# Mixture of experts behind attention: 624 slots per expert instead of 640

## Chip, cores and metric

One core of a Trainium2 chip runs the whole program. The metric is the device time of one execution in microseconds, as the median of several runs. Engines are named as the profile names them: PE (TensorE, with its weight loads PEld), DVE (VectorE), ACT (ScalarE), POOL (GpSimd) and SP (SyncE, which issues most DMAs).

## The reference

Three layers on 2304 tokens of 512 features: an attention that goes through 32 memory slots a head, a dense layer pair with an ELU between (512 to 2048 to 512), and a mixture of 8 experts with a noisy choice of two for each token.

```python
logits = x @ w_gate
noise_scale = np.log1p(np.exp(x @ w_noise))
noisy_logits = logits + noise_scale * noise
top2 = np.argpartition(-noisy_logits, 2, axis=1)[:, :2]
...
for e in range(E):
    for k in range(2):
        mask = top2[:, k] == e
        h = np.maximum(x[mask] @ w1[e], 0.0)          # 512 -> 1024
        out[mask] += top2_w[mask, k, None] * (h @ w2[e])  # 1024 -> 512
```

2304 tokens with two experts each make 4608 rows for 8 experts, 576 for one on average.

## The kernel before

The work is a flat list of units, each cut into slices of the hidden layer 128 wide (an iteration of the main loop). Units 0 to 3 are the dense layer pair on 576 tokens each, with 16 slices; the attention of the next block and the gating of the last one are woven between their matmuls. The rest are expert units with 8 slices. Experts 0 to 3 have two units each: a first one of 256 slots (E0A), filled from the first two blocks of tokens alone so that it can start early, and later one of the other CAP - 256 = 384 slots. Experts 4 to 7 have one unit of CAP = 640 slots each. The order is: four units of 256, four of 384, four of 640.

A slot is a row of a list in DRAM (`lst`, 2304 rows per expert, each a token number and a weight). The gating computes for every token its expert and its position there, and GpSimd scatters the pair into the list (line 643). The lists are first filled with numbers of junk rows (lines 842 to 846, 869), so that an unused slot reads and writes rows that nobody needs. `fetch` (L689) reads a unit's list and gathers its rows of x2d tile by tile, 128 slots each; `spread` (L710) turns each tile with four transposes on TensorE and splits it into a high and a low part for float32r (`halve`).

In each iteration `layer1` (L733) computes 128 hidden features for all slots of the unit: three terms (low x high, high x low, high x high) times four pieces of the 512 features, 12 matmuls for each stretch of at most 512 slots. A unit of 640 is cut in two halves of 320 (`splits`), so it has 24. `relu_` (L766) then splits the result again. Two iterations later (LAG) `layer2` (L775) takes each tile of 128 slots as the stationary operand and streams 512 output columns, three matmuls a tile, summed in one PSUM bank a tile over the 8 slices. `put_rows` (L790) scales a finished tile by the slots' weights and scatter-adds it to the output.

The order is written by hand; each engine runs its own queue in program order. SP loads the experts' weights as 1024 KB for two slices into three buffers, ACT and DVE split them into high and low parts. An expert that draws more tokens than CAP gets tiles of 128 slots behind everything, in a loop whose count is computed on the chip (`overflow_table`, and the loop at L987).

Of the kernel before, what the change touches and what calls it, by code (L numbers as in the profile page):

```python
# [9 lines left out]
F32 = mybir.dt.float32  # L10
F32R = mybir.dt.float32r
BF16 = mybir.dt.bfloat16
I32 = mybir.dt.int32
# [12 lines left out]
NT = N // P  # L26

BLOCKS = [(0, 4), (4, 5), (9, 4), (13, 5)]
CAP = 640
CT = CAP // P  # L30

NA, E0A = 4, 256
TPE = N // P
JUNK = 1024
NOV = 32
LAG = 2
# [4 lines left out]
def moe_stack_kernel(ctx, tc, phi, kv, q, wmlp, wgn, noise, wmoe, out):  # L41
# [16 lines left out]
    wxa = dr.tile([16, P, 512], F32, name="wxa")  # L58
    wxb = dr.tile([16, P, 512], F32, name="wxb")
    x2d = dr.tile([N + JUNK, DM], F32, name="x2d")  # L60
    lst = dr.tile([NE * N + P, 2], I32, name="lst")
    tabd = dr.tile([NOV, 2], I32, name="tabd")

    def bank(tag="px", bufs=1):
# [459 lines left out]
    def gating(blk, rows):  # L524
# [115 lines left out]
        for tt in range(nt):  # L640
            for k in range(2):
                pool.memset(tiny, 0.0)
                d = pool.indirect_dma_start(
                    out=lst[:NE * N], out_offset=bass.IndirectOffsetOnAxis(ap=slot[:, tt, k:k + 1], axis=0),
                    in_=rec[:, tt, k], in_offset=None)
# [6 lines left out]
    def overflow_table():  # L652
        tot = att["tot"]
        nti = sm.tile([1, NE], I32, tag="o_nti", name="o_nti")
        ntf = sm.tile([1, NE], F32, tag="o_ntf", name="o_ntf")
        end = sm.tile([1, NE], F32, tag="o_end", name="o_end")
        ge = sm.tile([1, NOV, NE], F32, tag="o_ge", name="o_ge")
        res = sm.tile([1, NOV, 2], F32, tag="o_res", name="o_res")
        tab = sm.tile([1, NOV, 2], I32, tag="o_tab", name="o_tab")
        cnt = sm.tile([1, 1], I32, tag="o_cnt", name="o_cnt")  # L660
        dve.tensor_scalar(ntf, tot[0:1], -float(CAP), 0.0, op0=OP.add, op1=OP.max)
        dve.tensor_scalar(ntf, ntf, 127.0, None, op0=OP.add)
        dve.tensor_copy(nti, ntf)
# [12 lines left out]
        dve.tensor_tensor(ge, ge, ntf[:, None, :].to_broadcast([1, NOV, NE]), op=OP.mult)  # L676
        dve.tensor_reduce(out=res[:, :, 1], in_=ge, axis=AX, op=OP.add)
        yield "light"

        dve.tensor_tensor(res[:, :, 1], ii, res[:, :, 1], op=OP.subtract)  # L680
        dve.tensor_scalar(res[:, :, 1], res[:, :, 1], float(CT), None, op0=OP.add)
        dve.scalar_tensor_tensor(res[:, :, 1], res[:, :, 0], float(TPE), res[:, :, 1], op0=OP.mult, op1=OP.add)
        dve.tensor_scalar(res[:, :, 0], res[:, :, 0], float(NE - 1), None, op0=OP.min)
        dve.tensor_scalar(res[:, :, 1], res[:, :, 1], float(NE * TPE - 1), None, op0=OP.min)
        dve.tensor_copy(tab, res)
        sp.dma_start(tabd[None], tab)
        att["cnt"] = cnt
        yield


    def fetch(n, wait=0, after=4):

        for _ in range(wait):
            yield "next"
        mp = moe["pool"]
        rows = JUNK + (BLOCKS[2][0] * P if n["early"] else N)
        ids = mp.tile([P, 5, 2], I32, tag="ids", name="ids", bufs=6)
        a, nt = n["e"] * N + n["s0"], n["nt"]
        sp.dma_start(ids[:, :nt], lst[a:a + nt * P].rearrange("(t p) c -> p t c", p=P))
        n["ids"] = ids  # L700
        n["xg"] = []
        for tt in range(nt):
            xg = mp.tile([P, DM], F32, tag="xg", name="xg", bufs=12)
            pool.indirect_dma_start(out=xg, out_offset=None, in_=x2d[:rows],  # L704
                                    in_offset=bass.IndirectOffsetOnAxis(ap=ids[:, tt, 0:1], axis=0))
            n["xg"].append(xg)
        for _ in range(after):
            yield "next"

    def spread(n):  # L710
        xt = n["x"]
        for tt in range(n["nt"]):
            bk = side_bank()
            for c in range(4):
                pe.transpose(bk[:, c * P:(c + 1) * P], n["xg"][tt][:, c * P:(c + 1) * P], ident)
            v = bk.rearrange("p (c n) -> p c n", c=4)
            hi = xt[0][:, :, tt * P:(tt + 1) * P]
            later(lambda a=(v, hi, xt[1][:, :, tt * P:(tt + 1) * P]): halve(*a))
            yield

    def new_x():
# [2 lines left out]
    def splits(u):  # L724
        if u["kind"] == "mlp":
            return [(0, S // 2), (S // 2, S // 2)]
        n = u["nt"] * P
        return [(0, n)] if n <= 512 else [(0, n // 2), (n // 2, n // 2)]

    def layer1(u, i, s0, n):  # L730
# [44 lines left out]
    def layer2(u, f, i, gh, gl, tiles=None):  # L775
        if f == 0:
            u["acc"] = [bank("acc%d" % t) for t in range(u["nt"])]
        if i >= NRAW:
            wh, wl = ready["b", i]
        for t in range(u["nt"]) if tiles is None else tiles:  # L780
            o = slice(t * P, (t + 1) * P)
            acc = u["acc"][t]
            if i < NRAW:
                pe.matmul(acc, gh.bitcast(F32)[:, o], raws["b", i], start=f == 0, stop=f == u["nf"] - 1)
                continue
            pe.matmul(acc, gl[:, o], wh, start=f == 0, stop=False)  # L786
            pe.matmul(acc, gh[:, o], wl, start=False, stop=False)  # L787
            pe.matmul(acc, gh[:, o], wh, start=False, stop=f == u["nf"] - 1)  # L788

    def put_rows(u, t, acc):  # L790
        r = rp.tile([P, DM], F32, tag="rows", name="rows")
        if u["kind"] == "mlp":
            if t % 2:
                act.activation(r, acc, AF.Copy)
            else:
                dve.tensor_copy(r, acc)
            a = JUNK + (BLOCKS[u["blk"]][0] + t) * P
            sp.dma_start(x2d[a:a + P, :], r)
            u["rows"].append(r)
        else:  # L800
            ids = u["ids"]
            wcol = ids.bitcast(F32)[:, t, 1:2]
            if t % 2:
                act.activation(r, acc, AF.Copy, scale=wcol)
            else:
                dve.tensor_scalar(r, acc, wcol, None, op0=OP.mult)  # L806
            pool.memset(tiny, 0.0)
            d = pool.indirect_dma_start(  # L808
                out=out, out_offset=bass.IndirectOffsetOnAxis(ap=ids[:, t, 0:1], axis=0), in_=r,
                in_offset=None, compute_op=OP.add)  # L810
# [14 lines left out]
    for f in at0[3:5]:  # L825
# [12 lines left out]
    dve.tensor_scalar(ecap, iota8, float(N), None, op0=OP.mult)  # L838
# [9 lines left out]
    moe_unit = lambda e, t, nt: dict(kind="moe", e=e, s0=t * P, nt=nt, nf=8, early=False)  # L848
    units += [moe_unit(e, 0, E0A // P) | dict(early=True) for e in range(NA)]
# [137 lines left out]
    with tc.For_i(0, nov, 1) as it:  # L987
        cur = mp.tile([1, 2], I32, tag="cur", name="cur")
        sp.dma_start(cur, tabd[bass.ds(it, 1), :])
        ev = sp.value_load(cur[0:1, 0:1], min_val=0, max_val=NE - 1)  # L990
        tv = sp.value_load(cur[0:1, 1:2], min_val=0, max_val=NE * TPE - 1)
        ids = mp.tile([P, 5, 2], I32, tag="ids", name="ids", bufs=6)
        sp.dma_start(ids[:, 0, :], lst.rearrange("(t p) c -> t p c", p=P)[bass.ds(tv, 1)].rearrange("a p c -> p (a c)"))
# [53 lines left out]
```

## Time and profile before

| what | value |
|---|---|
| median of 3 runs | 936.93 us (935.42 to 937.83) |
| profiled execution | 937.07 us, span 935.0 us, mean granted clock 0.979 |
| PE busy | 890.4 us (95%) |
| PE's weight loads | 736.7 us (79%) |
| DVE, ACT, POOL busy | 548.4, 455.1, 165.8 us |
| layer 2 of the experts, L786 to L788 | 3 x 544 matmuls, 218.3 + 213.2 + 213.0 us |
| layer 1 of the experts, L740 | 3 x 512 matmuls, 98.6 + 96.6 + 96.4 us |
| DMA | 153.12 MB, mean 164 GB/s |

The span is the time from the first to the last instruction; the run's own time is 2.1 us longer. Matmuls overlap: the busy time of one in the table (its mean) holds its latency, so what a matmul costs in a stream is read from the distance between two starts. The units of 256 slots begin at 443.8 us, those of 384 at 553.85, those of 640 at 691.89, and the last matmul starts at 925.00.

### The profile page before, as it was taken

What the parts mean: (1) busy time and instruction counts of PE and PEld (TensorE: products, weight loads), DVE (VectorE), ACT (ScalarE), POOL (GpSimd) and SP (SyncE); (2) the same over time, 40 slices, a digit from 0 to 9 for tenths busy, and PEclk for the clock granted to TensorE, in tenths of its full rate; (3) what the DMA queues carried; (4) which work ended last, traced back from release to release, by engine and by line L of the source; (5) the groups of instructions that cost most, each with busy time, mean ns of one, the idle gap of its engine ahead of it and who ended that gap; (6) DMA issues with size and microseconds to landing.
All of it is one profiled execution on the core that took longest, in us unless ns stands there. A gap on an engine that the chain in (4) does not pass through costs nothing. (4 is left out here: it accounts for less than half of the span.)

```text
span 935.0 us, 15299 instructions
## 1 busy us (share of the span) xinstructions
PE 890.4 (95%) x5810; PEld 736.7 (79%) x5810; DVE 548.4 (59%) x1189; ACT 455.1 (49%) x1003; POOL 165.8 (18%) x249
## 2 busy tenths in 40 slices
PE   6699999999989889999989999999999999999995
PEld 4366556787868667778878899999999999999994
DVE  4878977567577777578575654554544453442421
ACT  3676656545565556565554654444443242332310
POOL 0100100000000405033025312313304032030303
PEclk9689999999999999999999999999999999999998
DMA  8896549565652224342638966647546145162404
GB/s 318 301 360 230 181 149 357 212 237 158 210 205 90 69 72 136 118 151 53 230 96 160 309 204 191 169 138 212 145 172 180 58 113 168 46 147 74 72 3 57
DMA packets 69612, 153.12 MB, mean 164 GB/s; under 512 B 11170, under 2 KB 20130, under 8 KB 69538
## 3 DMA queue, kind: packets, MB, share of 16 engines
q1 hardware_dynamic: 59426, 131.12, 41.8%
q0 software_dynamic: 10112, 21.02, 11.6%
q8 instruction: 46, 0.75, 0.3%
q14 instruction: 28, 0.23, 0.1%
HBM read 119.42 MB, written 32.69 MB: 163 GB/s over the span
## 5 line engine op out<-in xcount | busy, mean ns | idle before, releaser
L786 PE MATMUL acc<-bh,gl 128*128 128x512 f32 x544 | 218.3, 401 | 0.6 <-DVE rows L806 0.5
L787 PE MATMUL acc<-bl,gh 128*128 128x512 f32 x544 | 213.2, 392 | 0.0
L788 PE MATMUL acc<-bh,gh 128*128 128x512 f32 x544 | 213.0, 391 | 0.0
L768 DVE SCALAR_TENSOR_TENSOR gl<-ph,gh 128x320 fp32r<-128x320 f32 (+2 forms) x128 | 62.9, 491 | 222.4 <-ACT gh L767 222.4
L470 ACT ACTIVATE bh<-raw 128x512 fp32r<-128x512 f32 x144 | 90.0, 625 | 78.1 <-PE acc L788 78.1
L788 PEld LDWEIGHTS acc<-bh,gh 128*128 128x128 f32 x544 | 102.3, 188 | 22.9
L767 ACT ACTIVATE gh<-ph 128x320 fp32r<-128x320 f32 (+2 forms) x128 | 55.8, 436 | 129.9 <-PE ph L740 129.9
L786 PEld LDWEIGHTS acc<-bh,gl 128*128 128x128 f32 x544 | 102.6, 189 | 18.7 <-DVE rows L806 1.2
L787 PEld LDWEIGHTS acc<-bl,gh 128*128 128x128 f32 x544 | 102.5, 188 | 16.6
L808 POOL DMA_INDIRECT out<-rows,ids x40 | 65.2, 1629 | 239.2 <-DVE rows L806 220.0
L476 DVE TENSOR_TENSOR bl<-raw,bh 128x512 fp32r<-128x512 f32 x144 | 98.7, 685 | 4.3 <-ACT bh L470 4.3
L740 PE MATMUL ph<-xl,ah 128*128 128x320 f32 (+2 forms) x512 | 98.6, 314 | 0.5 <-DVE gl L768 0.5
L740 PE MATMUL ph<-xh,ah 128*128 128x320 f32 (+2 forms) x512 | 96.6, 311 | 0.0
L740 PE MATMUL ph<-xh,al 128*128 128x320 f32 (+2 forms) x512 | 96.4, 310 | 0.0
L740 PEld LDWEIGHTS ph<-xl,ah 128*128 128x128 f32 x512 | 82.6, 189 | 6.7 <-DVE gl L768 0.9
L740 PEld LDWEIGHTS ph<-xh,ah 128*128 128x128 f32 x512 | 80.9, 189 | 0.0
L740 PEld LDWEIGHTS ph<-xh,al 128*128 128x128 f32 x512 | 80.7, 188 | 0.1
L740 PE MATMUL ph<-tl,fh 128*128 128x288 f32 x256 | 64.1, 332 | 11.1 <-DVE elu L754 5.5
L740 PEld LDWEIGHTS ph<-tl,fh 128*128 128x128 f32 x256 | 42.6, 195 | 37.4 <-issue 16.0
L476 DVE TENSOR_TENSOR al<-raw,ah 128x512 fp32r<-128x512 f32 x96 | 65.5, 682 | 0.0
L760 ACT ACTIVATE gh<-elu 128x576 fp32r<-128x576 f32 (+1 forms) x48 | 31.8, 662 | 66.6 <-DVE elu L754 66.6
L704 POOL DMA_INDIRECT xg<-x2d,ids x40 | 41.0, 1024 | 122.7 <-DMA ids<-lst 87.6
(219 smaller groups left out, 1290.8 us busy)
## 6 DMA issues: line engine op xcount, KB each, us to landing
raw<-in_wmoe SPq DMA_DIRECT2D x48, 1024.0 KB, 5.1
raw<-in_wmlp SPq DMA_DIRECT2D x32, 512.0 KB, 6.5
raw<-wxa SPq DMA_DIRECT2D x12, 1024.0 KB, 5.9
raw<-wxb SPq DMA_DIRECT2D x12, 1024.0 KB, 7.6
kv<-in_kv SPq DMA_DIRECT2D x8, 1024.0 KB, 11.9
out<-zrow SPq DMA_DIRECT2D x13, 512.0 KB, 8.7
q<-in_q SPq DMA_DIRECT2D x8, 576.0 KB, 8.0
x2d<-rows SPq DMA_DIRECT2D x18, 256.0 KB, 5.9
```

The source lines that it names most:

```text
L470: act.activation(ready[h, c][0], raws[h, c], AF.Copy)
L476: dve.tensor_tensor(lo, raws.pop((h, c)), hi.bitcast(F32), op=OP.subtract)
L704: pool.indirect_dma_start(out=xg, out_offset=None, in_=x2d[:rows], in_offset=bass.IndirectOffsetOnAxis(ap=ids[:, tt, 0:1], axis=0))
L740: pe.matmul(ph, w, x, start=k == 0, stop=k == len(terms) - 1)
L760: act.activation(gh[:, o], m, AF.Copy)
L767: act.activation(gh[:, o], ph, AF.Relu)
L768: dve.scalar_tensor_tensor(gl[:, o], ph, 0.0, gh[:, o].bitcast(F32), op0=OP.max, op1=OP.subtract)
L786: pe.matmul(acc, gl[:, o], wh, start=f == 0, stop=False)
L787: pe.matmul(acc, gh[:, o], wl, start=False, stop=False)
L788: pe.matmul(acc, gh[:, o], wh, start=False, stop=f == u["nf"] - 1)
L808: d = pool.indirect_dma_start(out=out, out_offset=bass.IndirectOffsetOnAxis(ap=ids[:, t, 0:1], axis=0), in_=r, in_offset=None, compute_op= ...
```

## The change

CAP becomes 624 = 4 x 128 + 112. The units of 640 slots become units of 624, in two halves of 312 and with a fifth tile of 112 slots; the units of 384 become 368, with a third tile of 112. Gathers, transposes, matmuls, scaling and scatters of these last tiles take 112 rows. The first units of 256 stay. The lists get LS = 2416 rows per expert, so that tiles of overflow, which now begin at slot 624, end inside the list of their expert; their start is kept in units of 16 rows (GR).

```diff
-CAP = 640
-CT = CAP // P
+CAP = 624
+LS = CAP + -(-(N - CAP) // P) * P
+GR = 16
...
-    lst = dr.tile([NE * N + P, 2], I32, name="lst")
+    lst = dr.tile([NE * LS, 2], I32, name="lst")
...
+    def size(u, t):
+        return min(P, u["n"] - t * P) if u["kind"] == "moe" else P
...
     def fetch(n, wait=0, after=4):
...
-        a, nt = n["e"] * N + n["s0"], n["nt"]
+        a, nt = n["e"] * LS + n["s0"], n["nt"]
...
-            pool.indirect_dma_start(out=xg, out_offset=None, in_=x2d[:rows],
-                                    in_offset=bass.IndirectOffsetOnAxis(ap=ids[:, tt, 0:1], axis=0))
+            m = size(n, tt)
+            pool.indirect_dma_start(out=xg[:m], out_offset=None, in_=x2d[:rows],
+                                    in_offset=bass.IndirectOffsetOnAxis(ap=ids[:m, tt, 0:1], axis=0))
...
     def spread(n):
...
-                pe.transpose(bk[:, c * P:(c + 1) * P], n["xg"][tt][:, c * P:(c + 1) * P], ident)
+                pe.transpose(bk[:, c * P:c * P + m], n["xg"][tt][:m, c * P:(c + 1) * P], ident[:m, :m])
...
     def splits(u):
...
-        n = u["nt"] * P
+        n = u["n"]
         return [(0, n)] if n <= 512 else [(0, n // 2), (n // 2, n // 2)]
...
     def layer2(u, f, i, gh, gl, tiles=None):
...
-            o = slice(t * P, (t + 1) * P)
-            acc = u["acc"][t]
+            m = size(u, t)
+            o = slice(t * P, t * P + m)
+            acc = u["acc"][t][:m]
...
     def put_rows(u, t, acc):
...
-            wcol = ids.bitcast(F32)[:, t, 1:2]
+            m = size(u, t)
+            r, acc, wcol = r[:m], acc[:m], ids.bitcast(F32)[:m, t, 1:2]
...
-    k = NE * TPE + 1
+    k = NE * LS // P
-    units += [moe_unit(e, E0A // P, (CAP - E0A) // P) for e in range(NA)]
-    units += [moe_unit(e, 0, CT) for e in range(NA, NE)]
+    units += [moe_unit(e, E0A, CAP - E0A) for e in range(NA)]
+    units += [moe_unit(e, 0, CAP) for e in range(NA, NE)]
...
     def overflow_table():
...
-        dve.tensor_scalar(res[:, :, 1], res[:, :, 1], float(CT), None, op0=OP.add)
+        dve.tensor_scalar(res[:, :, 1], res[:, :, 1], float(P // GR), float(CAP // GR), op0=OP.mult, op1=OP.add)
```

Every engine keeps its order; the shapes change. TensorE while expert 6 is worked on: the last two accumulators (tiles 3 and 4) of one iteration's layer 2, the transposes of expert 7's last tile of gathered rows (`xg`), and the first half of the next layer 1, before:

```order
L786 MATMUL acc_8395<-bh,gl 128x512
L787 MATMUL acc_8395<-bl,gh 128x512
L788 MATMUL acc_8395<-bh,gh 128x512
L786 MATMUL acc_8396<-bh,gl 128x512
L787 MATMUL acc_8396<-bl,gh 128x512
L788 MATMUL acc_8396<-bh,gh 128x512
L715 MATMUL px<-ident,xg 128x128 x4
L740 MATMUL ph<-xl,ah 128x320 x4
L740 MATMUL ph<-xh,al 128x320 x4
L740 MATMUL ph<-xh,ah 128x320 x4
```

The same place with the change, where the line numbers are 6 or 7 higher:

```order
L793 MATMUL acc_8395<-bh,gl 128x512
L794 MATMUL acc_8395<-bl,gh 128x512
L795 MATMUL acc_8395<-bh,gh 128x512
L793 MATMUL acc_8396<-bh,gl 112x512
L794 MATMUL acc_8396<-bl,gh 112x512
L795 MATMUL acc_8396<-bh,gh 112x512
L721 MATMUL px<-ident,xg 128x112 x4
L746 MATMUL ph<-xl,ah 128x312 x4
L746 MATMUL ph<-xh,al 128x312 x4
L746 MATMUL ph<-xh,ah 128x312 x4
```

Nothing moved: the fifth tile's three matmuls have 112 rows of output, its transposes 112 columns, and layer 1 streams 312 columns a half.

TensorE between two units of the other kind (experts 0 to 3): the transposes of a third tile, layer 1, and the first tile of layer 2, before:

```order
L715 MATMUL px<-ident,xg 128x128 x4
L740 MATMUL ph<-xl,ah 128x384 x4
L740 MATMUL ph<-xh,al 128x384 x4
L740 MATMUL ph<-xh,ah 128x384 x4
L786 MATMUL acc_6449<-bh,gl 128x512
L787 MATMUL acc_6449<-bl,gh 128x512
L788 MATMUL acc_6449<-bh,gh 128x512
```

With the change:

```order
L721 MATMUL px<-ident,xg 128x112 x4
L746 MATMUL ph<-xl,ah 128x368 x4
L746 MATMUL ph<-xh,al 128x368 x4
L746 MATMUL ph<-xh,ah 128x368 x4
L793 MATMUL acc_6449<-bh,gl 128x512
L794 MATMUL acc_6449<-bl,gh 128x512
L795 MATMUL acc_6449<-bh,gh 128x512
```

Nothing moved here either: 112 columns turned, 368 streamed in layer 1.

## Rows read from the trace of the kernel before

**Rows 1.** Busy us, share, instructions of each engine; granted clock in tenths by slice.

```profile
PE 890.4 (95%) x5810; PEld 736.7 (79%) x5810; DVE 548.4 (59%) x1189; ACT 455.1 (49%) x1003; POOL 165.8 (18%) x249
...
PEclk9689999999999999999999999999999999999998
```

**Rows 2.** Stretches: length, busy us (instructions) by engine, clock, DMA share, GB/s.

```profile
469.00:491.00 22.00, 19.41 (x114) 16.93 (x113) 17.17 (x52) 13.00 (x25) 5.68 (x15) 0.92 0.36 100
588.00:692.00 104.00, 104.00 (x546) 94.71 (x545) 53.39 (x89) 46.00 (x85) 29.08 (x32) 1.00 0.61 177
750.00:870.00 120.00, 120.00 (x684) 109.16 (x684) 46.99 (x83) 41.12 (x80) 21.68 (x25) 1.00 0.39 104
```

**Rows 3.** Waits, 553 to 915 us: total us, times, longest us.

```profile
DVE gl L768 <- ACT gh L767: 186.0, 96, 4.7
ACT gh L767 <- PE ph L740: 113.7, 95, 4.8
ACT bh L470 <- PE acc L788: 69.1, 40, 2.5
```

**Rows 4.** Waits of SyncE's queue, 553 to 915 us.

```profile
SPq L400 <- DVE bl L476: 286.9, 29, 15.6
```

**Rows 5.** TensorE in order, 640 slots: start, us, line, tiles, shape.

```profile
890.53 0.76 PE L740 MATMUL ph<-xl,ah 128*128 128x320 f32 x4
...
894.07 0.40 PE L786 MATMUL acc<-bh,gl 128*128 128x512 f32 x1
...
897.50 0.76 PE L740 MATMUL ph<-xl,ah 128*128 128x320 f32 x4
```

**Rows 6.** TensorE in order, 384 slots.

```profile
600.57 0.86 PE L740 MATMUL ph<-xl,ah 128*128 128x384 f32 x4
...
602.68 0.40 PE L786 MATMUL acc<-bh,gl 128*128 128x512 f32 x1
...
604.73 0.51 PE L740 MATMUL ph<-xl,ah 128*128 128x384 f32 x2
```

**Rows 7.** TensorE in order, 256 slots.

```profile
547.82 0.64 PE L740 MATMUL ph<-xl,ah 128*128 128x256 f32 x4
...
549.26 0.40 PE L786 MATMUL acc<-bh,gl 128*128 128x512 f32 x1
...
550.66 0.52 PE L740 MATMUL ph<-xl,ah 128*128 128x256 f32 x3
```

**Rows 8.** Weight loads by shape: count, busy us, mean ns, idle before.

```profile
L787 PEld LDWEIGHTS acc<-bl,gh 128*128 128x128 f32 x544 | 102.5, 188 | 16.6
...
L262 PEld LDWEIGHTS px<-kmT,q 128*128 128x128 f32 x80 | 9.5, 192 | 2.1 <-DMA q<-in_q 1.5 <-ACT kmT L221 0.3 <-issue 0.2
...
L262 PEld LDWEIGHTS acc<-kmT,q 128*64 128x64 f32 x24 | 1.6, 137 | 1.2 <-issue 1.1
...
L608 PEld LDWEIGHTS <-ones 128*128 128x128 bf16 x4 | 0.4, 100 | 0.0
```

**Rows 9.** TensorE in order, one tile of gathered rows turned.

```profile
746.74 0.60 PE L715 MATMUL px<-ident,xg 128*128 128x128 f32 x4
747.09 0.84 PE L740 MATMUL ph<-xl,ah 128*128 128x320 f32 x4
```

**Rows 10.** The end in order of time.

```profile
925.00 0.39 PE L788 MATMUL acc<-bh,gh 128*128 128x512 f32 x1
...
925.43 0.75 DVE L806 TENSOR_SCALAR rows<-acc,ids 128x512 f32<-128x512 f32 x1 [3.33 <-PE acc L788]
926.46 1.56 POOL L808 DMA_INDIRECT out<-rows,ids  x1 [0.49 <-DVEq L987]
```

**Rows 11.** DMA issues, 915 us to the end: count, us to landing.

```profile
out<-rows,ids POOLq DMA_INDIRECT x5, 4.9
```

**Rows 12.** The page's DMA issues: count, KB each, us to landing.

```profile
raw<-in_wmlp SPq DMA_DIRECT2D x32, 512.0 KB, 6.5
```

**Rows 13.** GpSimd in order, first 60 us.

```profile
24.95 1.05 POOL L291 TENSOR_TENSOR sb<-sb,ssu 128x512 f32<-128x512 f32 x1 [22.28 <-DVE ssu L289]
```

More of the change, by code (lines that the diff above doesn't have):

```diff
@@ L28 @@
 BLOCKS = [(0, 4), (4, 5), (9, 4), (13, 5)]
-CAP = 640
-CT = CAP // P
+CAP = 624
+LS = CAP + -(-(N - CAP) // P) * P
+GR = 16
 NA, E0A = 4, 256
-TPE = N // P
 JUNK = 1024
@@ L643, in gating @@
                 d = pool.indirect_dma_start(
-                    out=lst[:NE * N], out_offset=bass.IndirectOffsetOnAxis(ap=slot[:, tt, k:k + 1], axis=0),
+                    out=lst, out_offset=bass.IndirectOffsetOnAxis(ap=slot[:, tt, k:k + 1], axis=0),
                     in_=rec[:, tt, k], in_offset=None)
@@ L680, in overflow_table @@
         dve.tensor_tensor(res[:, :, 1], ii, res[:, :, 1], op=OP.subtract)
-        dve.tensor_scalar(res[:, :, 1], res[:, :, 1], float(CT), None, op0=OP.add)
-        dve.scalar_tensor_tensor(res[:, :, 1], res[:, :, 0], float(TPE), res[:, :, 1], op0=OP.mult, op1=OP.add)
+        dve.tensor_scalar(res[:, :, 1], res[:, :, 1], float(P // GR), float(CAP // GR), op0=OP.mult, op1=OP.add)
+        dve.scalar_tensor_tensor(res[:, :, 1], res[:, :, 0], float(LS // GR), res[:, :, 1], op0=OP.mult, op1=OP.add)
         dve.tensor_scalar(res[:, :, 0], res[:, :, 0], float(NE - 1), None, op0=OP.min)
-        dve.tensor_scalar(res[:, :, 1], res[:, :, 1], float(NE * TPE - 1), None, op0=OP.min)
+        dve.tensor_scalar(res[:, :, 1], res[:, :, 1], float((NE * LS - P) // GR), None, op0=OP.min)
         dve.tensor_copy(tab, res)
@@ L712, in spread @@
         for tt in range(n["nt"]):
-            bk = side_bank()
+            bk, m = side_bank(), size(n, tt)
             for c in range(4):
-                pe.transpose(bk[:, c * P:(c + 1) * P], n["xg"][tt][:, c * P:(c + 1) * P], ident)
-            v = bk.rearrange("p (c n) -> p c n", c=4)
-            hi = xt[0][:, :, tt * P:(tt + 1) * P]
-            later(lambda a=(v, hi, xt[1][:, :, tt * P:(tt + 1) * P]): halve(*a))
+                pe.transpose(bk[:, c * P:c * P + m], n["xg"][tt][:m, c * P:(c + 1) * P], ident[:m, :m])
+            v = bk.rearrange("p (c n) -> p c n", c=4)[:, :, :m]
+            hi, lo = (t[:, :, tt * P:tt * P + m] for t in xt)
+            later(lambda a=(v, hi, lo): halve(*a))
             yield
@@ L808, in put_rows @@
             d = pool.indirect_dma_start(
-                out=out, out_offset=bass.IndirectOffsetOnAxis(ap=ids[:, t, 0:1], axis=0), in_=r,
+                out=out, out_offset=bass.IndirectOffsetOnAxis(ap=ids[:m, t, 0:1], axis=0), in_=r,
                 in_offset=None, compute_op=OP.add)
@@ L837, in moe_stack_kernel @@
               allow_small_or_imprecise_dtypes=True)
-    dve.tensor_scalar(ecap, iota8, float(N), None, op0=OP.mult)
+    dve.tensor_scalar(ecap, iota8, float(LS), None, op0=OP.mult)
     pool.iota(ii, pattern=[[1, NOV]], base=0, channel_multiplier=0, allow_small_or_imprecise_dtypes=True)
     pool.iota(tokid, pattern=[[P, NT]], base=JUNK, channel_multiplier=1)
-    k = NE * TPE + 1
+    k = NE * LS // P
     pre = rp.tile([P, DM], F32, tag="rows", name="rows").bitcast(I32)[:, :2 * k].rearrange("p (t c) -> p t c", c=2)
@@ L847, in moe_stack_kernel @@
     units = [dict(kind="mlp", blk=k, nt=BLOCKS[k][1], nf=16) for k in range(4)]
-    moe_unit = lambda e, t, nt: dict(kind="moe", e=e, s0=t * P, nt=nt, nf=8, early=False)
-    units += [moe_unit(e, 0, E0A // P) | dict(early=True) for e in range(NA)]
-    units += [moe_unit(e, E0A // P, (CAP - E0A) // P) for e in range(NA)]
-    units += [moe_unit(e, 0, CT) for e in range(NA, NE)]
+    moe_unit = lambda e, s0, n: dict(kind="moe", e=e, s0=s0, n=n, nt=-(-n // P), nf=8, early=False)
+    units += [moe_unit(e, 0, E0A) | dict(early=True) for e in range(NA)]
+    units += [moe_unit(e, E0A, CAP - E0A) for e in range(NA)]
+    units += [moe_unit(e, 0, CAP) for e in range(NA, NE)]
     late = 4 + NA
@@ L990, in moe_stack_kernel @@
         ev = sp.value_load(cur[0:1, 0:1], min_val=0, max_val=NE - 1)
-        tv = sp.value_load(cur[0:1, 1:2], min_val=0, max_val=NE * TPE - 1)
+        tv = sp.value_load(cur[0:1, 1:2], min_val=0, max_val=(NE * LS - P) // GR)
         ids = mp.tile([P, 5, 2], I32, tag="ids", name="ids", bufs=6)
-        sp.dma_start(ids[:, 0, :], lst.rearrange("(t p) c -> t p c", p=P)[bass.ds(tv, 1)].rearrange("a p c -> p (a c)"))
+        sp.dma_start(ids[:, 0, :], lst.rearrange("(t p) c -> t p c", p=GR)[bass.ds(tv, P // GR)]
+                     .rearrange("t p c -> (t p) c"))
         xg = mp.tile([P, DM], F32, tag="xg", name="xg", bufs=12)
```

## Prediction

> **What bounds the kernel now.** I read the busy table and the slices first, then the stretches of time, the waits in them, and at last TensorE's rows one after the other. TensorE is busy for 890.4 of 935.0 us, and its granted clock is at the upper level nearly throughout [rows 1]. The change touches only what follows 553 us, the expert units with a slot count of 384 and of 640, so those stretches decide. In 588 to 692 us (384 slots) and in 750 to 870 us (640 slots) TensorE is busy for the whole stretch at a granted clock of 1.00, while VectorE and ScalarE are busy for half of it or less and the DMA engines for 0.61 and 0.39 of it [rows 2]. The waits agree: between 553 and 915 us ScalarE waits 113.7 us for layer 1's matmuls and 69.1 us for layer 2's, VectorE waits 186.0 us for ScalarE [rows 3], and the queue of weight loads waits 286.9 us for VectorE to free a buffer [rows 4], so weights are early, not late. TensorE has no wait of note there. Time that leaves TensorE's stream between 553 and 925 us therefore leaves the span; time that leaves another engine does not.
>
> **What one iteration consists of.** An iteration is one 128-wide slice of the hidden layer. In a 640-slot unit, layer 1 starts at 890.53 and layer 2 at 894.07, the next layer 1 at 897.50 [rows 5]: 24 matmuls of 320 columns in 3.54 us (147.5 ns each), then 15 of 512 columns in 3.43 us (229 ns each), 6.97 us in all. In a 384-slot unit 12 matmuls of 384 columns take 602.68 - 600.57 = 2.11 us (175.8 ns each), the iteration 4.16 us [rows 6]. In a 256-slot unit 12 of 256 columns take 549.26 - 547.82 = 1.44 us (120 ns each) [rows 7]. From 256 to 384 columns a matmul grows by 55.8 ns, 0.436 ns a column; from 256 to 512 (229 ns) by 109 ns, 0.426 ns a column. I take 0.43 ns. Between 320 and its neighbours the same comes out, so there is no step between widths: a matmul costs what it streams and about 10 to 15 ns beside.
>
> **Layer 1 narrower.** A 640-slot unit becomes two halves of 312 instead of 320: 24 matmuls x 8 columns x 0.43 = 83 ns an iteration. A 384-slot unit becomes 368: 12 x 16 x 0.43 = 83 ns. There are 4 units of each kind with 8 iterations, 64 iterations: 64 x 0.083 = 5.3 us, all of it on TensorE's stream. By the full clock alone (1 / 2.4 = 0.417 ns) it would be 5.1 us, by the steeper pair (320 to 384: 28.3 ns over 64 columns, 0.44) 5.4. The relu and subtraction that follow get shorter by the same share, but they are waiting engines and give nothing.
>
> **Layer 2 with a last tile of 112 rows.** It streams 512 columns as before; only the stationary operand has 112 columns. These are 3 x 64 = 192 matmuls. The trace has no such shape with float32r. The nearest loads: 188 ns for 128 columns of float32r, 192 ns for 128 columns of plain float32, 137 ns for 64 columns, so 0.86 ns a column [rows 8]. A load starts while the matmul before it streams, and the next start comes 229 ns on, so a load of 188 ns or less lies under it. I take 0. Bounds: if the load were exposed, 16 columns less would give 192 x 14 ns = 2.6 us; if a 112-wide load ran at some slower path and were fully exposed (one more 188 ns each), it would cost 192 x 0.188 = 36 us.
> The bfloat16 load of 128 columns takes 100 ns, the float32r one 188, as long as plain float32 [rows 8]. The Trainium skill (TensorE: Matmul & The Clock Gate, section on Fast Weight Load) says that the fast load is used where the weights number 128 and the type is not FP32; by its words a 112-wide load would lose it, and this is the rule that speaks against the change. The rows say that float32r loads like float32 and has nothing to lose; the sum by the row is 0, by the rule a loss that the third rival prices.
>
> **The gathered rows' transposes.** Of each of the 8 units one tile is turned with 112 instead of 128 streamed columns, 4 transposes each, 32 in all. Four of them hold TensorE for 747.09 - 746.74 = 0.35 us, 88 ns each [rows 9]. If all of that scaled, 32 x 88 / 8 = 0.35 us go; if it is the load of the 128-wide tile that sets it, nothing. I take 0.2.
>
> **The end.** The last matmul starts at 925.00, VectorE scales the last tile from 925.43 for 0.75 us, GpSimd issues its scatter-add from 926.46 for 1.56 us [rows 10], and such a scatter lands 4.9 us after its issue [rows 11]. VectorE's part has the same 512 columns and stays. The issue and the transfer carry 112 rows for 128: if all scaled by an eighth, 0.2 + 0.6 = 0.8 us; if both are fixed, nothing. I take 0.2.
>
> **Edits at no cost.** The fill of the lists grows from 145 to 151 columns on GpSimd and in one DMA of 145 KB; its two GpSimd instructions run before a wait of 22.28 us there [rows 13], and only the scatters into the lists, behind the first block's gating, need the result. If that cover were gone, 4% of two short instructions would show. The overflow table's arithmetic has the same count of one-row instructions, on a VectorE that waits half the time. Gathers and scatters of 112 rows are shorter, on GpSimd, which waits for rows and lists. No instruction changes its place on any engine, and no wait is added; SyncE's queue keeps its order too.
>
> **Sum.** 5.3 + 0 + 0.2 + 0.2 = 5.7 us. Against the profiled execution, 937.07 us (a span of 935.0 and 2.1 around it), that is 931.4. The median of the three runs shown, 936.93, is 0.14 lower, within their spread of 2.4 us, so I leave it at 931.4, 0.6% below.
>
> **Rivals.**
> *The second half starts badly.* The 640-slot units' second half now starts at column 312 instead of 320; no row shows a stream that starts off the old grid. If that takes 3 ns or so from each matmul, those units gain nothing: 5.7 - 2.65, so 934.0. For it speaks nothing in the trace; against it the even cost per column.
> *Something else holds the iteration.* If weights or VectorE set the 4.16 or 6.97 us, narrower matmuls only make TensorE wait: about 936.5. Against it stand the full TensorE stretches [rows 2] and the early weights [rows 4].
> *The 112-wide load is slow (the other side).* Place: the 192 matmuls of layer 2's last tile. The load has 229 ns of cover against 188 ns today, so it needs to be over 41 ns longer before anything shows. From about 30 ns exposed each (5.7 us / 192) the gain is gone, from 45 ns the kernel is slower by over 0.3%; at 100 ns each (half a load) 19.2 us are lost: 945. At the far bound, 967. Against it: the equal times of float32 and float32r, and that 64 columns load faster than 128.
> *An overflow tile runs.* With 624 slots an expert that draws more gets a tile of its own behind everything. It needs, one after the other, its table entry, its list and its gather (some 5 us each, priced as the scatter in [rows 11]), a first 512 KB of weights (6.5 us, [rows 12]) and a scatter (4.9): at least 26 us, so 957 or more. Against it: the reference's own top-2 on the inputs it draws gives 588, 553, 571, 566, 576, 611, 543 and 600 tokens, none over 624; experts 0 to 3 have at least 267 in the first two blocks, so none is padded there.
>
> **How the numbers follow.** Forecast 0.80; half start 0.07; another holder 0.06; slow load 0.03; overflow 0.02; and 0.02 for more gain than forecast (layer 2's 2.6 us). The forecast's own range: its terms give a gain of 5.1 to 6.6 us, 930.5 to 932.0, and the clock adds its share: in 469 to 491 us, before the changed part, the granted clock was 0.92 [rows 2], about 3.5 us at the lower level (1.2 GHz) and so 1.8 us lost; whether such a stretch falls there again is open. Added to both ends, that is 928.7 to 933.8. To take in the half-start case, at 934.0 with half a microsecond around it, the range given goes up to 934.6. About 0.3%, 2.8 us, is what a measurement of this kernel can tell from no change: under 934.1 counts as faster. Half of the first rival falls there: faster 0.80 + 0.02 + 0.04 = 0.86, same 0.03 + 0.06 = 0.09, slower 0.03 + 0.02 = 0.05.
>
> **What would show it.** Iterations of 6.89 us instead of 6.97 and of 4.08 instead of 4.16, each without a wait on TensorE; 312-column matmuls 144 ns apart in both halves and 368-column ones 169 ns; the three matmuls of a 112-row tile 229 ns apart like their neighbours; the end, from the last matmul on, 0 to 0.8 us shorter. I am wrong if the second half's matmuls are slower than the first's, if the rows of a 112-row tile are wider apart than 229 ns, or if the code of the overflow loop appears after the last scatter.

## The result and the profile after

The median went from 936.93 us (933.79 to 943.08, 9 runs) to 928.57 us (926.03 to 933.68, 9 runs), ratio 0.9896 with a 95% interval of 0.9865 to 0.9928. The forecast was 931.4 with a range from 928.7: the direction is right, the time lies 0.13 us below the range. The profiled execution took 927.74 us, 9.3 less than the one before.

The page after has nearly the same shares as before [rows 1]; TensorE's busy time fell by 8.4 us, and one slice near the start shows a higher granted clock (the third digit, 9 where it was 8):

```profile
PE 882.0 (95%) x5810; PEld 726.4 (78%) x5810; DVE 547.1 (59%) x1189; ACT 454.2 (49%) x1003; POOL 166.3 (18%) x249
...
PEclk9699999999999999999999999999999999999998
```

That is the first hint that not all of the gain comes from the changed units. The start of the first matmul of each kind of unit divides the span. Before: first unit of 256 at 443.82, of 384 at 553.85, of 640 at 691.89, last matmul 925.00. After: 440.25, 549.42, 685.52, 915.86. So the 9.0 us of the span are 3.6 in the dense stage and 0.9 in the units of 256, where nothing was changed, 1.9 in the units of 384, 2.8 in those of 640; and the end is 0.1 longer. The stretches of the changed units as windows (start:end, length, busy us and instructions by engine, granted clock, DMA share, GB/s), first before, then after:

```profile
553.80:691.90 138.10, 138.10 (x726) 125.99 (x724) 70.55 (x118) 61.78 (x114) 35.51 (x39) 1.00 0.59 174
691.90:925.00 233.10, 233.10 (x1325) 212.12 (x1322) 91.25 (x177) 76.57 (x148) 45.40 (x53) 1.00 0.37 93
```

```profile
549.40:685.50 136.10, 136.10 (x725) 122.30 (x724) 69.86 (x118) 61.22 (x114) 35.89 (x39) 1.00 0.60 175
685.50:915.90 230.40, 230.40 (x1325) 207.61 (x1323) 90.43 (x177) 76.08 (x148) 44.72 (x53) 1.00 0.38 94
```

TensorE fills them as before [rows 2], at the upper level (2.4 GHz) throughout. Nothing that became faster opened a wait there.

An iteration of a 624-slot unit in TensorE's order (start, duration, line, tiles, shape), against [rows 5]:

```profile
888.63 0.73 PE L746 MATMUL ph<-xl,ah 128*128 128x312 f32 x4
...
890.33 0.74 PE L746 MATMUL ph<-xl,ah 128*128 128x312 f32 x4
...
892.07 0.39 PE L793 MATMUL acc<-bh,gl 128*128 128x512 f32 x1
...
895.51 0.73 PE L746 MATMUL ph<-xl,ah 128*128 128x312 f32 x4
```

24 matmuls of 312 in 3.44 us (3.54 before), layer 2 in 3.44 (3.43 before), 6.88 us in all: as forecast. The two halves are not alike, though. The first takes 1.70 us (141 ns a matmul), the second, which starts at column 312, takes 1.74 (145 ns), and so it is in the steady iterations of all six traces with this shape. Before, the halves stood at 147.8 and 146.7 ns. A slower second half is one of the signs by which the prediction would call itself wrong; here the two together come to 143.0 ns a matmul, under the forecast of 144, and e6 below tries another start.

The 368-slot units show something else. Two iterations of the same trace, in the second and in the fourth unit, against [rows 6]:

```profile
603.76 0.85 PE L746 MATMUL ph<-xl,ah 128*128 128x368 f32 x4
...
605.83 0.39 PE L793 MATMUL acc<-bh,gl 128*128 128x512 f32 x1
...
673.00 0.84 PE L746 MATMUL ph<-xl,ah 128*128 128x368 f32 x4
...
675.00 0.40 PE L793 MATMUL acc<-bh,gl 128*128 128x512 f32 x1
```

The same 12 matmuls take 2.07 us in one (173 ns each, start to start) and 2.00 in the other (166 ns); 2.11 before. TensorE waits in neither, and the iteration takes 4.15 or 4.05 us where 4.08 was forecast.

The end, against [rows 10]: from the last matmul on 10.1 us (10.0 before). The scatter's issue takes 1.49 us for 1.56, and it starts later after the scaling than before (0.40 us instead of 0.28). Over all profiles this end takes 10.0 to 10.7 us with the kernel before and 10.1 to 10.7 with the change.

```profile
915.86 0.39 PE L795 MATMUL acc<-bh,gh 128*112 128x512 f32 x1
916.18 0.62 POOL L815 MEMSET tiny<- 1x1 f32 x1
916.29 0.75 DVE L814 TENSOR_SCALAR rows<-acc,ids 112x512 f32<-112x512 f32 x1 [3.35 <-PE acc L795]
917.44 1.49 POOL L816 DMA_INDIRECT out<-rows,ids  x1 [0.64 <-DVEq L995]
```

### The profile page after: what moved, and what is told of

Its sections match the earlier page's. It is cut to its first block, busy times and chain, and to the rows that moved or that the text cites. A ratio compares the mean times of both kernels' runs of the same rounds, so it can differ in the third digit from the quotient of the medians.

```text
span 926.0 us, 15299 instructions
## 1 busy us (share of the span) xinstructions
PE 882.0 (95%) x5810; PEld 726.4 (78%) x5810; DVE 547.1 (59%) x1189; ACT 454.2 (49%) x1003; POOL 166.3 (18%) x249
## 5 line engine op out<-in xcount | busy, mean ns | idle before, releaser
L793 PE MATMUL acc<-bh,gl 128*128 128x512 f32 (+1 forms) x544 | 217.5, 400 | 0.5 <-DVE rows L814 0.5
L795 PE MATMUL acc<-bh,gh 128*128 128x512 f32 (+1 forms) x544 | 213.5, 392 | 0.0
L794 PE MATMUL acc<-bl,gh 128*128 128x512 f32 (+1 forms) x544 | 213.3, 392 | 0.0
L774 DVE SCALAR_TENSOR_TENSOR gl<-ph,gh 128x312 fp32r<-128x312 f32 (+2 forms) x128 | 61.8, 483 | 218.2 <-ACT gh L773 218.2
L795 PEld LDWEIGHTS acc<-bh,gh 128*128 128x128 f32 (+1 forms) x544 | 101.2, 186 | 23.5
L793 PEld LDWEIGHTS acc<-bh,gl 128*128 128x128 f32 (+1 forms) x544 | 101.5, 187 | 18.7 <-DVE rows L814 1.1
L794 PEld LDWEIGHTS acc<-bl,gh 128*128 128x128 f32 (+1 forms) x544 | 101.5, 186 | 18.0
L746 PE MATMUL ph<-xl,ah 128*128 128x312 f32 (+2 forms) x512 | 97.3, 312 | 0.0
L746 PE MATMUL ph<-xh,ah 128*128 128x312 f32 (+2 forms) x512 | 94.7, 307 | 0.0
L746 PE MATMUL ph<-xh,al 128*128 128x312 f32 (+2 forms) x512 | 94.7, 307 | 0.0
```

What stands on the lines that cost most here:

```text
L746: pe.matmul(ph, w, x, start=k == 0, stop=k == len(terms) - 1)
L774: dve.scalar_tensor_tensor(gl[:, o], ph, 0.0, gh[:, o].bitcast(F32), op0=OP.max, op1=OP.subtract)
```

## The experiments

**Whose are the 4.4 us ahead of the changed units?** The first set took four kernels on one chip: before against itself, the lists alone, the shapes alone, and the change.

The lists alone (e1) and the shapes alone (e2):

```diff
 e1, against the change:
-CAP = 624
-LS = CAP + -(-(N - CAP) // P) * P
+CAP = 640
+LS = 2416
 e2, against the change:
-LS = CAP + -(-(N - CAP) // P) * P
+LS = N          # 2304 rows per expert, as before
...
```

In e2 the spare rows behind the lists and the bounds that hang on their length go back with it.

> The kernel before, unchanged, against itself. Theory A (chance): what the change gained ahead of 553 us, 3.6 us in the dense stage and 0.9 us in the units of 256, is the place of the stretches at the lower TensorE clock, which differs from run to run. Then runs of one and the same kernel spread by some 8 us, the longer ones at a lower mean clock, and where two profiles of this kernel differ in the dense stage they differ by the time at the lower clock. Theory B (systematic): the stage before 553 us takes the same time in every run of one kernel, within 1 us; the two profiles here would agree at 443.8 us for the first expert unit within 1 us.

> 640 slots as before, only with the longer lists (2416 rows per expert) and overflow tiles that begin at multiples of 16. Theory A: ratio to before 1.000, within its interval. Theory B, with the lists as the cause of what was gained ahead of the expert units: about 4 us faster, 0.996, and the first expert unit near 440 us.

> 624 slots with the shapes of the change, but the lists of before (2304 rows per expert). Theory A: the whole effect of the shapes is in here, 4.6 to 5.5 us, ratio 0.9945 at the same mean clock, as for the full change. Theory B with the lists: the same 5 us, while the full change on this chip gains 8 to 9.

> The changed kernel once more, on the same chip as the other three. Theory A: 0.9945 (5 us), lower than the 0.9896 seen first, and at the same mean clock as the runs of before beside it 5 us apart. Theory B: 0.990 again, with the mean clock of its runs above that of the runs of before.

Ratios to before (median 946.89 there): before itself 0.9984 (0.9957 to 1.0011), lists alone 0.9997 (0.9970 to 1.0024), shapes alone 0.9956 (0.9928 to 0.9983), change 0.9928 (0.9896 to 0.9961). The 44 runs of before spread from 943.8 to 954.7, and the longer ones have the lower mean granted clock. A straight line through all runs (a level for each kernel, one slope for the clock) gives 0.47 us for each 0.001 of mean clock, and at a clock of 0.980: before 946.8 and 946.3, lists 946.8, shapes 941.3, change 941.6, each give or take 0.3 to 0.6. So on this chip the shapes are all of it, 5.1 us, and the lists cost and give nothing that these runs could tell from zero.

In the profile of e0 the first expert unit comes at 450.4 us, but a stall of that chip, told at the end, lies ahead of it, so theory B was not settled by it. The gain of 8 to 9 on the first chip stayed open, and the same kernels ran in three more sets. Theory A calls the excess chance; theory D looks for a part ahead of the changed units that only the kernel with 640 slots has.

> The kernel before once more, since the stage ahead of 553 us is still open: at the same mean clock the change was worth 5.1 us in one set of runs and 8 to 9 in two others. Theory A (chance of the runs, clock and single stalls ahead of the expert units): ratio 1.000 within its interval, and a dense stage that differs from profile to profile at the places where the clock is low or one iteration stalls, nowhere else. Theory D (a part ahead of 553 us that only the kernel with 640 slots has): the dense stage and the units of 256 take over 2 us more here than with the change beside it, at one and the same iteration each time.

> 640 slots with the longer lists and the overflow tiles at multiples of 16, again. Theory A: 1.000, at most 1 us from before at the same mean clock. Theory D with the lists as the cause: 3 to 4 us faster, 0.996.

> The change again. Theory A: over both sets together 5 us at the same mean clock; here 4 to 6.5. Theory D: 8 to 9 again. In the trace, from the first 368-column matmul to the last matmul: 366.0 to 366.4, against 371.15 before, under either.

> The kernel before, for its own stage ahead of 553 us. The dense stage took 406.4 to 406.7 us in five profiles of kernels with the change's lists on chips without the long iteration 43 (7.65 us), 409.19 in the one profile of before there, and 415 to 423 on chips with it (13.5 us or more). Theory A (chance): where iteration 43 takes 7.65 us, before comes out at 406.5 too when the same stretches at the lower clock fall on it. Theory D: over 409 again.

> 640 slots with the longer lists, beside before and the change. Theory A: ratio 1.000, dense stage as before's. Theory D with the lists: 0.996 and a dense stage about 3 us shorter than before's.

> The change, beside before. Theory A: 5 us at the same mean clock, 4 to 6.5. Theory D: 8 to 9 where iteration 43 takes 7.65 us, 5 where it takes 13.5 or more.

> The change, beside 616 slots and before: 4.5 to 6 us faster than before at the same mean clock, as on the other chips, ratio 0.9940 give or take 0.003.

| set | before, median | change, median | ratio (95%) | at a mean clock of 0.980 |
|---|---|---|---|---|
| first | 936.93 | 928.57 | 0.9896 (0.9865 to 0.9928) | not known for before |
| e3 | 946.89 | 940.39 | 0.9928 (0.9896 to 0.9961) | 946.8, 941.6 |
| e12 | 951.38 | 947.16 | 0.9945 (0.9916 to 0.9974) | 949.0, 944.0 |
| e16 | 935.94 | 930.70 | 0.9943 (0.9920 to 0.9966) | 938.1, 931.5 |
| e19 | 947.78 | 942.11 | 0.9932 (0.9903 to 0.9961) | 947.1, 941.9 |

The copies of before gave 0.9990 (e10) and 1.0001 (e14), the lists alone 0.9990 (e11) and 0.9996 (e15). In e16 before runs at 935.9, as on the first chip, and the change gains 5.2 us, not 8 to 9. The four later ratios have a mean of 0.9937, which makes 931.0 of 936.93. At equal mean clock the change is worth 5.0 to 6.6 us.

Theory D does not hold, although one of its signs came. It expected the dense stage of before (from its first matmul to the first of the expert units) at over 409 us again in e14, and it was 410.7 there, against 406.4 in e15 and e16. But 410.5 us stand in e17, which has the change's lists and narrower units, and on the chip of e10 to e13 it is the other way round: 414.9 us for before (e10), 422.9 for the change (e12). Profile against profile, the 63 distances between the dense iterations agree within 0.3 us in all but nine places, in all twenty profiles; the whole spread is in those. One of the nine, the iteration that starts near 269 us, by windows in e14 (before), e0 (before), e12 (change) and e16 (change):

```profile
268.85:279.15 10.30, 10.30 (x106) 8.28 (x106) 7.40 (x30) 5.21 (x14) 1.61 (x4) 0.70 0.32 104
268.89:277.20 8.31, 7.79 (x107) 5.91 (x107) 7.40 (x30) 4.65 (x14) 1.61 (x4) 1.00 0.38 129
268.84:279.05 10.21, 10.21 (x107) 8.25 (x107) 7.40 (x30) 5.21 (x14) 1.61 (x4) 0.71 0.32 105
268.83:277.14 8.31, 7.82 (x106) 5.91 (x106) 7.40 (x30) 4.63 (x14) 1.61 (x4) 1.00 0.44 139
```

Either kernel takes 8.3 us at a granted clock of 1.00 (third number from the end) or 10.2 to 10.3 at 0.70 or 0.71, as the run has it. So theory A stands for the traces. The first pair differs in the same way. Two places of its dense stage, before and then after; each pair is the same work:

```profile
34.60:62.00 27.40, 22.06 (x89) 14.79 (x89) 24.32 (x51) 21.29 (x47) 0.00 (x0) 0.69 0.89 317
271.30:280.30 9.00, 9.00 (x106) 7.34 (x106) 7.39 (x30) 5.21 (x14) 1.61 (x4) 0.81 0.32 119
```

```profile
33.50:59.30 25.80, 20.43 (x89) 14.09 (x89) 24.29 (x51) 21.30 (x47) 0.00 (x0) 0.74 0.89 318
268.40:276.80 8.40, 7.86 (x107) 5.95 (x107) 7.46 (x30) 4.68 (x14) 1.61 (x4) 1.00 0.34 126
```

The granted clock was 0.69 and 0.81 in one execution, 0.74 and 1.00 in the other, and with it go 1.6 and 0.6 of the 3.6 us; another 1.1 lie ahead of the first dense matmul (34.63 and 33.50 us). The stretch from the first 384-column matmul to the last matmul, in contrast, is 371.15 us within 0.01 in every profile of before and of the lists alone (before, e0, e1, e10, e11, e14, e15), on three chips at least.

That the medians of the first comparison got their further 3 us by the same chance is likely, but not shown: its interval ends at 0.9928, just short of the later mean, and the clocks of its runs of before are not known. Sets of runs do shift as a whole. On one chip and at the same mean clock (0.982) before has a median of 939.64 us beside e4 to e9 and of 935.94 beside e14 to e17; and e4, whose changed stretch is longer than before's by the trace, ran at 931.95 us in its single run, 7.7 under the median of before beside it.

**Does the narrow tile cost anything?** Only layer 2's last tile, with its scaling and its scatter, at 112 rows:

```diff
     def fetch(n, wait=0, after=4):
...
-            m = size(n, tt)
+            m = P
...
     def spread(n):
...
-            bk, m = side_bank(), size(n, tt)
+            bk, m = side_bank(), P
...
     def splits(u):
...
-        n = u["n"]
+        n = u["nt"] * P
```

> Only the last tile of layer 2 (and its scaling and scatter) has 112 rows; layer 1, gathers and transposes stay at 384 and 640 slots. Read from the trace, from the first 384-column matmul to the last matmul: 371.15 us before (138.04 + 233.11). Theory P (the narrow stationary operand is free, as predicted): 371.15 within 0.2. Rival L (it changes the rhythm of the loads): the 512-column matmuls of that tile more than 2 ns further apart or closer than 229 ns, 0.4 us or more in all, or layer 1's 384-column matmuls take another rhythm than 175.6 ns.

> Only the last tile of layer 2 at 112 rows, lists as in the change. Its stretch from the first 384-column matmul to the last matmul was 371.54, 0.4 more than before. Theory A: no faster than before, 0 to +0.5 us at the same mean clock. Theory D with the lists: 3 us faster than before.

TensorE's first 384-column matmul and the last matmul of e4:

```profile
547.94 0.95 PE L746 MATMUL ph<-xl,ah 128*128 128x384 f32 x4
```

```profile
919.48 0.39 PE L795 MATMUL acc<-bh,gh 128*112 128x512 f32 x1
```

919.48 - 547.94 = 371.54, in e13 the same: 0.4 us more than before, spread over 64 iterations (6 ns each). Theory P's bound of 0.2 is missed, rival L's 0.4 just reached; layer 1 keeps 175.5 ns, and the 6 ns are in layer 2. In the timed runs e13 is 0.9987 (0.9954 to 1.0020). The weight loads of the change by shape (x count, busy us, mean ns, idle before), against [rows 8]:

```profile
L794 PEld LDWEIGHTS acc<-bl,gh 128*128 128x128 f32 x480 | 90.3, 188 | 14.6
L794 PEld LDWEIGHTS acc<-bl,gh 128*112 128x112 f32 x64 | 11.2, 175 | 3.4
```

The load got shorter by 13 ns for 16 columns, so the rival of a slow load falls. (The same lines serve the dense layer: 224 of the 480 loads, and of the 544 that the table of the kernel before gives to the experts, are its own.) By the Trainium skill (TensorE: Matmul & The Clock Gate, section on Fast Weight Load) a load of fewer than 128 weights would lose the fast path; here it had none to lose, with 188 ns at 128 columns as against 192 for plain float32 [rows 8]. Layer 1 narrower with full tiles in layer 2 was not tried, since the tile would read columns that nothing had written; its share is taken as the difference.

**Does the second half's start matter?**

```diff
-        return [(0, n)] if n <= 512 else [(0, n // 2), (n // 2, n // 2)]
+        return [(0, n)] if n <= 512 else [(0, 320), (320, n - 320)]
```

> 624 slots cut into 320 + 304 instead of 312 + 312, the second half starting where it started before. The stretch of the last four units was 233.11 us before and 230.34 with 312 + 312. Theory P (0.43 ns a column, the start does not matter): the same sum of columns, 230.3 within 0.3. Rival S (steps: a matmul's cost goes by the rhythm that a width falls into, not by its columns): 320 stays at 147.0 ns, 304 is off the line (not 140.1 ns), and the stretch differs from 230.3 by more than 0.5. Rival M (a start off the old grid cost something): the 304-wide half is below the line and the stretch shorter than 230.3.

```profile
890.87 0.76 PE L746 MATMUL ph<-xl,ah 128*128 128x320 f32 x4
...
892.64 0.72 PE L746 MATMUL ph<-xl,ah 128*128 128x304 f32 x4
...
894.33 0.39 PE L793 MATMUL acc<-bh,gl 128*128 128x512 f32 x1
```

320 takes 147.5 ns a matmul, 304 takes 140.8, and the stretch of the last four units is 230.26 us against 230.34. The start does not matter for the sum, so the rival of the half that starts badly falls. The halves of one unit differ without following the start: 140.0 and 137.8 ns with 304 columns (e17), 143.1 and 142.3 with 308 (e7), 142.3 and 150.8 with 316 (e9). What sets this is open.

**Is it columns or rhythms?** Eight widths in one kernel (e9), then 616 slots for all experts (e7, and beside the change e18):

```diff
 e9, against the change:
-    units += [moe_unit(e, E0A, CAP - E0A) for e in range(NA)]
-    units += [moe_unit(e, 0, CAP) for e in range(NA, NE)]
+    units += [moe_unit(e, E0A, (352, 336, 376, 360)[e]) for e in range(NA)]
+    units += [moe_unit(e, 0, (592, 616, 608, 632)[e - NA]) for e in range(NA, NE)]
 e7 and e18, against the change:
-CAP = 624
-LS = CAP + -(-(N - CAP) // P) * P
-GR = 16
+CAP = 616
+LS = 2416
+GR = 8
```

> Eight widths of layer 1 in one kernel, by units that just hold this input's counts: 352, 336, 376 and 360 slots for the second units of experts 0 to 3, then halves of 296, 308, 304 and 316. Theory P (a straight line through 320 at 147.0 and 384 at 175.6 ns, 0.447 a column): 336: 154.2, 352: 161.3, 360: 164.9, 376: 172.0; 296: 136.3, 304: 139.8, 308: 141.6, 316: 145.2, each in one rhythm. Rival S (steps): some widths stand in two rhythms several ns apart, as 368 did (173.3 in 16 groups of 32, 166 in the others), and neighbours can cost the same.

> 616 slots per expert (halves of 308, second units of 360, last tiles of 104 rows; overflow tiles at multiples of 8): still over the 611 of the fullest expert. Theory P by the line: 2.6 us less than with 624 in the stretch (363.7 against 366.3), and at the same mean clock 7.5 us less than before. Rival S: 360 stands in the rhythm of 173 ns or of 166 and the stretch gains under 1.5 us or over 3.5 against 624. In the plain medians, before and this differ by 7.5 us give or take 2 for the clock.

> 616 slots beside 624 on the same chip. By the traces its changed stretch is 365.2 us against 364.9 to 366.4 with 624 (the second units of 368 stand in one of two rhythms by chance), and its end is some 0.5 longer. Theory R (rhythms decide, not columns): within 1.5 us of the change at the same mean clock. Theory P (0.43 ns a column, 64 iterations of 41 ns): 2.6 us faster than the change.

Distance of two starts within layer 1 in ns, means of an iteration without its first two, by width (e9; 312 and 368 from the change, 320 and 384 from before); "line" is the straight line through 320 and 384 columns:

| columns | 296 | 304 | 308 | 312 | 316 | 320 | 336 | 352 | 360 | 368 | 376 | 384 |
|---|---|---|---|---|---|---|---|---|---|---|---|---|
| ns | 136.7 | 138.6 | 142.6 | 142.3 | 146.3 | 147.0 | 153.4 | 159 or 167 | 166.4 | 166 or 173.3 | 173.1 | 175.6 |
| line | 136.3 | 139.8 | 141.6 | 143.4 | 145.2 | 147.0 | 154.2 | 161.3 | 164.9 | 168.5 | 172.0 | 175.6 |

The line holds within 1.6 ns for most, but 352 and 368 stand in one of two rhythms, and neighbours share one: an iteration of 376 in e9 and one of 360 in e7 show the two rhythms between which 368 chooses. The 352-column units go from one rhythm to the other and back with every iteration (e9, e17).

```profile
637.05 0.85 PE L746 MATMUL ph<-xl,ah 128*128 128x376 f32 x4
...
639.13 0.39 PE L793 MATMUL acc<-bh,gl 128*128 128x512 f32 x1
```

```profile
598.18 0.83 PE L746 MATMUL ph<-xl,ah 128*128 128x360 f32 x4
...
600.18 0.39 PE L793 MATMUL acc<-bh,gl 128*128 128x512 f32 x1
```

2.08 and 2.00 us for 12. In seven traces with 368 columns 16 of 28 units ran in the slow rhythm. A unit starts with the transposes of its last tiles; one to three iterations after them it has settled, by its fifth iteration at the latest, and then keeps its rhythm until the next unit's transposes. The same kernel has three slow units in one trace (after, e19), two in others (e3, e12), none in e16; its four units take 136.1, 135.6 to 135.7 and 134.65 us accordingly. 616 slots give 134.57 + 230.62 us, 365.2 in both traces where the line says 363.7: theory P is out by 1.5 us. The halves of 308 columns even make the longer iteration, 6.91 us against 6.88 with 312, by layer 2 (e7):

```profile
886.54 0.73 PE L746 MATMUL ph<-xl,ah 128*128 128x308 f32 x4
...
889.97 0.40 PE L793 MATMUL acc<-bh,gl 128*128 128x512 f32 x1
...
893.45 0.73 PE L746 MATMUL ph<-xl,ah 128*128 128x308 f32 x4
```

Layer 1 takes 3.43 us, layer 2 takes 3.48 instead of 3.44, with as many columns streamed. The same goes for the halves of 316 in e9, whose iteration takes 6.99 to 7.00 us against 6.97 with 320.

Timed beside each other, 616 has 0.9935 (0.9911 to 0.9958) and the change 0.9932 (0.9903 to 0.9961); at a clock of 0.980, 941.2 and 941.9, each give or take 0.5. The fewer columns no longer pay, so no version here is shown to beat the change. e7's 0.9894 (0.9870 to 0.9919) had no change beside it; like the first comparison it lies some 3 us beyond what the traces account for, and why is as open.

**What does an overflow tile cost?** CAP = 608, LS = 2416: the expert with 611 rows gets one tile behind everything.

> 608 slots per expert: one expert draws 611, so one tile of overflow runs behind everything, and the rest is narrower (halves of 304, second units of 352). The prediction's rival put such a tile at 26 us or more. Stretch to the last matmul of the last unit by the widths measured: second units some 32 us each, halves of 139 to 140 ns a matmul: 363 to 365 us against 366.3. So about 25 us slower than with 624 slots.

The median is 952.59 (two runs), 1.0168 to before (1.0116 to 1.0219) and 21.9 us above the change beside it. The end in order of time:

```profile
912.19 0.40 PE L795 MATMUL acc<-bh,gh 128*96 128x512 f32 x1
...
915.39 1.02 POOL L1004 DMA_INDIRECT xg<-x2d,ids  x1 [0.30 <-issue]
...
919.93 1.09 PE L1008 MATMUL px<-ident,xg 128*128 128x128 f32 x4 [7.35 <-DMA xg<-x2d,ids]
...
942.23 1.12 PE L1020 MATMUL acc<-raw,elu 128*128 128x512 f32 x2 [0.43 <-ACT elu L1019]
943.39 0.75 DVE L1022 TENSOR_SCALAR rows<-acc,ids 128x512 f32<-128x512 f32 x1 [30.02 <-PE acc L1020]
944.54 1.57 POOL L1023 DMA_INDIRECT out<-rows,ids  x1 [28.12 <-DVE rows L1022]
```

The last matmul of the units is at 912.19, the end at 952.9: 40.7 us instead of 10.1. The tile costs 30.6 us, the bound of 26 held, and the narrower units pay back 5.1 to 6.6 of it: they took 359.9 us where 363 to 365 were expected and the change takes 365.0 (e16) to 366.4. The first of its eight steps takes 4.3 us, the others 2.4; they alternate between TensorE and ScalarE (TensorE waits 0.43 us for ScalarE at each turn), and a wait for weights shows once (0.58 us).

## Why the prediction was wrong

*The failing step is the clock's share of the range, 1.8 us.* The prediction said that "the granted clock was 0.92 [rows 2], about 3.5 us at the lower level (1.2 GHz) and so 1.8 us lost; whether such a stretch falls there again is open", and added 1.8 us to both ends. It looked only at the stretch just ahead of the changed units. The dense stage has more such stretches, which the slices showed near the start [rows 1], and they come and go from run to run: in single profiles without the stall told at the end the untouched dense stage takes 406.4 to 410.7 us, a spread of 4.3, and the untouched units of 256 take 107.7 to 111.2. So the first 384- or 368-column matmul comes at 549.7 to 555.1 us in the profiles of e14, e15, e16 and at 553.85 and 549.42 in the first pair, 4.4 us apart. Single runs of one kernel lie 6 us from their median in the first comparison and up to 9.6 in a later one, and by its own interval a comparison of nine runs with nine carries about 3 us of chance on either side. With 3 us instead of 1.8 the range had held the time. The forecast itself stands by the four later sets: 5.7 us less was forecast, their ratios of 0.9928 to 0.9945 make 5.2 to 6.7 us of 936.93.

*Layer 1 narrower:* forecast 5.3 us, half in each kind of unit. The 624-slot units gave 2.8 with their tile's cost, in every trace (233.11 to 230.3). The 368-slot units gave 1.9 to 3.4 where 2.65 was forecast, by how many units fall into the slow rhythm. The sum, 4.7 to 6.2, has the forecast near its middle; the straight line behind it, "a matmul costs what it streams and about 10 to 15 ns beside", is right on the mean and wrong as a rule ("no step between widths"). That the sum came out is in part luck: 312 columns lie 1.1 ns under the line, 368 lie 2.5 under it or 4.8 over it.

*The tile of 112 rows:* forecast 0, measured +0.4 us. *The transposes:* forecast 0.2, and the trace agrees with the larger bound: four of a 112-wide tile hold TensorE for 0.32 us (697.97 to 698.29 in the trace after) where four of a 128-wide one hold it for 0.35, some 39 ns a tile before rounding and 0.3 us for eight tiles. They are part of the sums above. *The end:* forecast 0.2 less, measured 0.1 more in the profile: the issue is 0.07 shorter, the rest varies by more. *The lists:* forecast nothing, measured nothing in three sets (e1, e11, e15).

*The rivals:* the half that starts badly fell with e6, another holder of the iteration with the full TensorE stretches, the slow load with e4; the overflow tile did not run, and its price of at least 26 us was right (30.6, e17). Two prices were added up wrongly. Second-half matmuls that lose 3 ns each cost 12 x 32 x 3 ns = 1.2 us, not 2.65; and a load that loses 19.2 us makes 931.4 + 19.2 = 950.6 us, not 945. Neither enters the forecast, but the range goes up to 934.6 for the first.

## What to carry to other kernels

Where one engine fills a stretch, compare that stretch in two traces, first instruction to last, before trusting medians: here it repeats to 0.01 us with the kernel before on three chips, and to 1.5 us with the change, while whole runs of one kernel spread by 7 to 14 us. Take the spread of the untouched part from several profiles or runs, not from the one stretch that looks odd, and put it into the range. Before cutting a width further, read the distance between two matmul starts at the new width: 312 and 308 columns, or 376 and 368 in its slow rhythm, cost the same. Read the whole iteration too, since with 308 columns layer 2 took back more than layer 1 had saved. And price the case that a tighter limit brings on: one tile too many costs six times what 16 slots save.

## What the runs showed that was not expected

*One stream, two rhythms.* The 368-column matmuls, with no wait on TensorE, run 173 or 166 ns apart for the rest of a unit once it has settled, and which of the two differs from run to run. In the slow rhythm every distance but the first is 173 or 174 ns, in the fast one they go up and down between 160 and 171. Why is open; all that the traces show is that the choice falls within three iterations of the unit's transposes.

*A stall on some chips.* On three of the chips (e0 to e3, e10 to e13, e18 and e19) iteration 43 of the dense stage, counted from 0, takes 13.4 us or more, on the chip of e4 to e9 and e14 to e17 and in the first pair 7.65, in every profile. Each of the three ran in one set alone, so chip and set are not told apart. TensorE in e0, while the gating's small matmuls run and GpSimd scatters into the lists:

```profile
317.23 0.37 PE L533 MATMUL acc<-wgs,x2T 128*32 128x16 f32 x20 [0.26 <-DVE fl L137]
318.13 0.22 PE L533 MATMUL acc<-wgs,x2T 128*32 128x16 f32 x2 [0.53 <-issue]
...
320.95 0.32 PE L533 MATMUL acc<-wgs,x2T 128*32 128x16 f32 x6 [1.15 <-issue]
...
323.62 0.63 PE L787 MATMUL acc<-bl,gh 128*128 128x512 f32 x1
324.04 0.63 PE L788 MATMUL acc<-bh,gh 128*128 128x512 f32 x1
```

and in the first profile of before:

```profile
319.60 0.45 PE L533 MATMUL acc<-wgs,x2T 128*32 128x16 f32 x32
...
321.71 0.39 PE L787 MATMUL acc<-bl,gh 128*128 128x512 f32 x1
321.94 0.40 PE L788 MATMUL acc<-bh,gh 128*128 128x512 f32 x1
```

The 32 small matmuls that come in one piece there trickle in over 4 us, TensorE waiting for nothing that the profile shows ("issue"); after these gaps its clock is near the lower level (512 columns 0.42 us apart, not 0.23) for the twelve matmuls of layer 2 that follow, by the window of e0 at a granted clock of 0.56:

```profile
323.60:329.00 5.40, 5.40 (x46) 3.84 (x45) 1.02 (x4) 1.26 (x3) 0.00 (x0) 0.56 0.85 66
```

Stall and clock together make the 6 to 7 us. Iteration 50 is longer there too, 8.4 to 13.0 us against 6.6 to 6.9, and the two make up most of the 7 to 15 us by which the medians of before differ between the chips. The cause of the stall was not tried.
